# Attention into a mixture of experts on one core: gating of a batch cut into blocks and spread over later pairs' steps

## The chip, the cores and the metric

The kernel runs on one NeuronCore of a Trainium2 chip. The metric is the device time in microseconds (us); lower is better. The kernel before was run 14 times: median 584.34 us, from 579.7 to 599.25. One more execution was recorded by the hardware profiler: 582.62 us, of which 580.8 us lie between its first and its last instruction (the span).

## The reference

```python
q_d, k_d, v_d = (x.reshape(B, H, Sd, 4, D).mean(axis=3) for x in (q, k, v))
out_up = np.repeat(softmax_attn(q_d, k_d, v_d), 4, axis=2)
mask = np.abs(pos[:, None] - pos[None, :]) < 4
out_local = softmax_attn(q, k, v, mask)
x = (out_up + out_local)          # as 4608 rows (batch, position) of 512 (head, dim)
logits = x @ w_gate
e_idx = np.argmax(logits, axis=1)
gate_w = softmax(logits)[e_idx]
eom = sigmoid(x @ w_output_gate)
out[row] = gate_w * eom[row, e_idx] * (relu(x[row] @ w1[e_idx]) @ w2[e_idx])
```

There are 8 batches, 8 heads, 576 positions and 64 dims; 8 experts, with w1 512x1024 and w2 1024x512. Two attentions are added for each head: one over means of four positions, repeated four times, and one over a band of seven positions. The sum, all heads of a position side by side, is a row of 512; each row goes to the one expert that its logits choose.

## The kernel before, in words

Values go through TensorE as float16, the sensitive ones as a high half and a low half (the rest of the value after the high half), so that products come out nearly exact.

**Pairs.** The unit of attention is a pair of heads, u = 0 to 31; four pairs make a batch. For a pair, `load` (L178) issues six DMAs on SP's queue (q, k and v of two heads) and has POOL cast q and k to float16 (L187). `prep` (L195) makes v's halves `vh` on ACT (L201) and `vl` on DVE (L202), turns q and k on TensorE into the PSUM tiles `t1` and `t2f` (L214, L218), copies them out (L220, L221 on DVE, L223 on ACT), and forms v's means of four in `pd` (L229 to L232), with halves by ACT (L234) and DVE (L235). `scores_a` and `scores_b` (L248, L262) write a pair's masked scores to PSUM; `soft` (L241) makes the exponential's high half `eh` and the exponential itself on ACT (L244, L245), and the low half `el` on DVE (L246). `values` (L277) multiplies one head's exponentials with v in 27 matmuls into `po` (L298), and DVE divides by the row sums into the batch's tile `xo` (L301, L302).

**Gating.** When a batch's four pairs are through, its 576 rows lie in `xo` as five blocks of 120 rows (neighbours overlap). `gate1` (L304) repeats the coarse result four times by SBUF to SBUF DMAs on SP's queue (`up`, L313 to L316), adds it on POOL (L319), rounds to float16 on ACT (`xh`, L320) and takes the low half on POOL (`xl`, L321), each in one instruction of 120x2560 for all five blocks (for the last batch, one per block). `gate2` (L324) turns each block on TensorE into a PSUM tile `tp` (L331, L333), copies it out (L336 on ACT or L338 on DVE) and multiplies with the gate weights into a PSUM tile `lg` (L340, L343). `gate3` (L345) finds each row's expert and its rank there in some twenty small instructions, mostly on DVE, and POOL scatters the rows to DRAM, one indirect DMA for each block (L402). L392, in `gate3`, writes row numbers beside the rows.

**Experts.** From L509, one expert after another: its rows are read back, turned, and sent through two matmuls; POOL scatters the results to the output. Weights come on POOL's queue (`load_weights`, L158) into three sets of buffers; those of the first three experts are requested during attention, at u = 10, 16 and 22, each behind a one-element copy (L162, L163) that reads `vh` of that pair.

**PSUM.** [...] `T` has two slots shared by `t1`, `t2f`, `pd`, `lg`, `tp` and `gate3`'s rank tile; `SA` and `SB` (scores) take two banks each; `O` has two slots of one bank, one head's `po` each. `lg` keeps a slot of `T` from the first block of `gate2` until L350 has read it.

**Order.** [...] The compiler's scheduler sets that order: of the instructions that it takes to be ready, by its own model of time, the one written first. It also brings forward what is written much later, when that is ready. The loop at L423 writes, for each u: loads of u+3, `scores_a(u+1)`, head 0 of `values(u)`, `scores_b(u+1)`, `prep(u+2)`, head 1 of `values(u)`, and in the four steps after a batch `gate1`, `gate2` and `gate3` of that batch in the first, second and third.

Of the kernel before, what the change touches and what calls it, by code (L numbers as in the profile page):

```python
# [34 lines left out]
def kernel(  # L35
# [83 lines left out]
    for i in range(3):  # L119
        t_vh = cst.tile([128, 2, NB, 66], F16, tag=f"vh{i}")  # L120
        nc.vector.memset(t_vh[:, :, :, 64:66], 0.25)
        vh_s.append(t_vh)
        t_vd = cst.tile([128, 2, 2, 66], F16, tag=f"vd{i}")
        nc.vector.memset(t_vd[:, :, :, 64:66], 0.25)
        vdh_s.append(t_vd)
# [32 lines left out]
    def load_weights(e, after=None):  # L158
        w1sb = wpool.tile([128, 4, F], F16, tag="w1")
        w2sb = wpool.tile([128, NG, Dm], F16, tag="w2")  # L160
        if after is not None:
            nc.gpsimd.tensor_copy(w1sb[0:1, 0, 0:1], after)  # L162
            nc.gpsimd.tensor_copy(w2sb[0:1, 0, 0:1], after)  # L163
        nc.gpsimd.dma_start(w1sb, moe_w1[e].rearrange("(c p) f -> p c f", p=128))
        nc.gpsimd.dma_start(w2sb, moe_w2[e].rearrange("(g p) j -> p g j", p=128))
        wts[e] = (w1sb, w2sb)
# [9 lines left out]
    st = {}  # L176

    def load(u):  # L178

        b, hp = u // NP, u % NP  # L180
        s16 = []
        for i, src in enumerate((q, k)):
# [3 lines left out]
            t16 = sbA.tile([96, 6, 2 * D], F16, tag=f"qk16{i}")  # L186
            nc.gpsimd.tensor_copy(t16, f.rearrange("p m h d -> p m (h d)"))  # L187
            s16.append(t16)
# [4 lines left out]
        st[u] = {"s16": s16, "vf": vf}  # L193

    def prep(u):  # L195

        d = st[u]
        s16, vf = d.pop("s16"), d.pop("vf")
        vh = vh_s[u % 3]
        vl = sbA.tile([128, 2, NB, D], F16, tag="vl", bufs=3)  # L200
        nc.scalar.activation(vh[:, :, :, 0:D], vf, AF.Copy, scale=VS)  # L201
        nc.vector.scalar_tensor_tensor(vl, in0=vf, scalar=VS, in1=vh[:, :, :, 0:D],  # L202
                                       op0=ALU.mult, op1=ALU.subtract)
# [11 lines left out]
        for i in range(2):  # L215
            for m in range(6):
                c = 96 + SD * i + 24 * m
                nc.tensor.matmul(t2f[:, c:c + 24], lhsT=s16[i][:, m, :], rhs=pb[0:96, 0:24],  # L218
                                 start=True, stop=True)
        nc.vector.tensor_copy(qkT[:, 0:n1], t1[:, 0:n1])  # L220
        nc.vector.tensor_copy(qkT[:, n1:2 * S], t2[:, 0:2 * S - n1])  # L221
        qkd = sbA.tile([128, 2 * SD], F16, tag="qkd", bufs=3)
        nc.scalar.copy(qkd, t2f[:, 96:96 + 2 * SD])  # L223
        vdh = vdh_s[u % 3]
        vdl = sbA.tile([128, 2, 2, D], F16, tag="vdl", bufs=3)
        pd = psA.tile([128, 2, 2, D], F32, tag="T", bufs=2)
# [4 lines left out]
        for i, m in enumerate((vh, vl)):  # L231
            nc.tensor.matmul(pd[:, 1], lhsT=pv[:, NB - 1, 128:256], rhs=m[:, :, NB - 1, 0:D],  # L232
                             start=(i == 0), stop=(i == 1), skip_group_check=True)
        nc.scalar.copy(vdh[:, :, :, 0:D], pd)  # L234
        nc.vector.tensor_tensor(vdl, pd, vdh[:, :, :, 0:D], op=ALU.subtract)  # L235
        d.update(qT=qkT[:, 0:S], kT=qkT[:, S:2 * S], qd=qkd[:, 0:SD], kd=qkd[:, SD:2 * SD],
                 vh=vh, vl=vl, vdh=vdh, vdl=vdl)
        d["eh"] = sbA.tile([128, 2, ND], F16, tag="eh", name="eh", bufs=2)
        d["el"] = sbA.tile([128, 2, ND], F16, tag="el", name="el", bufs=2)

    def soft(d, ps, c0, c1):  # L241
# [4 lines left out]
        nc.vector.tensor_tensor(d["el"][:, :, c0:c1], ps[:, :, 0:n], d["eh"][:, :, c0:c1], op=ALU.subtract)  # L246

    def scores_a(u):  # L248
        d = st[u]
        ps = psA.tile([128, 2, 512], F32, tag="SA")  # L250
# [9 lines left out]
        soft(d, ps, 0, NA)  # L260

    def scores_b(u):  # L262
        d = st[u]
        ps = psA.tile([128, 2, 512], F32, tag="SB")
# [10 lines left out]
        soft(d, ps, NA, ND)  # L275

    def values(u, h, xo):  # L277

        d = st[u]
        eh, el = d["eh"][:, h], d["el"][:, h]  # L280
        hh = 2 * (u % NP) + h
        po = psA.tile([128, NB + 2, 65], F32, tag="O", bufs=2)
        mms = []
        for e_, hi in ((eh, True), (el, False)):
            for t in range(NB):
                c = slice(Q0[t], Q0[t] + 128)
                mms.append((po[:, t, 0:65], e_[:, c], d["vh"][:, h, t, 0:65]))
                if hi:
                    mms.append((po[:, t, 0:D], e_[:, c], d["vl"][:, h, t, :]))
            for g, q0 in ((NB, 0), (NB + 1, 16)):  # L290
                for kc, kn in ((0, 128), (1, 16)):
                    c = slice(S + SD * kc + q0, S + SD * kc + q0 + 128)
                    mms.append((po[:, g, 0:65], e_[0:kn, c], d["vdh"][0:kn, kc, h, 0:65]))
                    if hi:
                        mms.append((po[:, g, 0:D], e_[0:kn, c], d["vdl"][0:kn, kc, h, :]))

        for i, (o, a, m) in enumerate(mms):
            nc.tensor.matmul(o, lhsT=a, rhs=m, start=(i == 0), stop=(i == len(mms) - 1),  # L298
                             skip_group_check=True)
        rs = sbA.tile([128, NB + 2], F32, tag="rs", bufs=3)  # L300
        nc.vector.reciprocal(rs, po[:, :, 64])  # L301
        nc.vector.tensor_tensor(xo[:, :, D * hh:D * hh + D], po[:, :, 0:D], _bc(rs, D), op=ALU.mult)  # L302

    def gate1(b, parts):  # L304

        xo = xo_s[b]
        xh, xl = xh_s[b % 2], t_xl
        up = sbA.tile([BR, NB, Dm], F32, tag="up", bufs=1)
        for t in range(NB):
# [3 lines left out]
            nc.sync.dma_start(up[0:4 * n, t, :], _ap(src, [src.ap[0], [0, 4], [1, Dm]]))  # L313
            if n < 30:
                src = xo[112:128, NB + 1, :]
                nc.sync.dma_start(up[4 * n:BR, t, :], _ap(src, [src.ap[0], [0, 4], [1, Dm]]))  # L316
        for t0, t1 in parts:
            x = xo[0:BR, t0:t1, :]
            nc.gpsimd.tensor_tensor(x, x, up[:, t0:t1], op=ALU.add)  # L319
            nc.scalar.copy(xh[0:BR, t0:t1, 0:Dm], x)  # L320
            nc.gpsimd.tensor_tensor(xl[0:BR, t0:t1], x, xh[0:BR, t0:t1, 0:Dm], op=ALU.subtract)  # L321

    def gate2(b, ts):
        xh, xl = xh_s[b % 2], t_xl  # L324
        if ts[0] == 0:
            lg_s[b] = psA.tile([128, NB, 4 * E], F32, tag="T", name="lg", bufs=2)
        lg = lg_s[b]
        for t in ts:
            tp = psA.tile([128, 8, 128], F16, tag="T", bufs=2)
            for c in range(4):  # L330
                nc.tensor.transpose(tp[:, c, :], xh[:, t, 128 * c:128 * c + 128], id16)  # L331
            for c in range(4):
                nc.tensor.transpose(tp[:, 4 + c, :], xl[:, t, 128 * c:128 * c + 128], id16)  # L333
            xT = sbA.tile([128, 8, 128], F16, tag="xT")
            if t % 2:
                nc.scalar.copy(xT, tp)  # L336
            else:
                nc.vector.tensor_copy(xT, tp)  # L338
            for c in range(4):
                nc.tensor.matmul(lg[:, t, :], lhsT=xT[:, c, :], rhs=wg[:, c, :],  # L340
                                 start=(c == 0), stop=False, skip_group_check=True)
            for c in range(4):
                nc.tensor.matmul(lg[:, t, 0:2 * E], lhsT=xT[:, 4 + c, :], rhs=wg[:, c, 0:2 * E],  # L343
                                 start=False, stop=(c == 3), skip_group_check=True)

    def gate3(b):
        xh, w9, lg = xh_s[b % 2], w9_s[b % 2], lg_s.pop(b)
        P = BR
        lg2 = sbA.tile([P, NB, 4 * E], F32, tag="lg2")
        nc.scalar.copy(lg2, lg[0:P])  # L350
# [50 lines left out]
        for t in range(NB):  # L401
            ins = nc.gpsimd.indirect_dma_start(  # L402
                out=xs_dram.ap(), out_offset=bass.IndirectOffsetOnAxis(ap=pos[:, t:t + 1], axis=0),
                in_=xh[0:P, t, :].bitcast(I32), in_offset=None, bounds_check=E * REG - 1, oob_is_err=False)
# [3 lines left out]
    xo_s, lg_s = {}, {}  # L408
    NU = B * NP
    late = {10: 0, 16: 1, 22: 2}  # L410

    def late_weights(u):

        if u in late:
            load_weights(late[u], st[u]["vh"][0:1, 0, 0, 0:1])

    for u in range(3):
        load(u)
    for u in range(2):
        prep(u)  # L420
    scores_a(0)
    scores_b(0)
    for u in range(NU + 5):  # L423
        b, hp = u // NP, u % NP
        if u == 1:
            prefill()
        if u + 3 < NU:
            load(u + 3)
        if u + 1 < NU:
            scores_a(u + 1)  # L430
        if u < NU:
            if hp == 0:
                xo_s[b] = sbA.tile([128, NB + 2, Dm], F32, tag="xo", name="xo")
            values(u, 0, xo_s[b])
        if u + 1 < NU:
            scores_b(u + 1)
        if u + 2 < NU:
            prep(u + 2)
        if u < NU:
            values(u, 1, xo_s[b])  # L440
            late_weights(u)
        gb = b - 1
        last = gb == B - 1
        if gb >= 0:
            if hp == 0:
                gate1(gb, [(t, t + 1) for t in range(NB)] if last else [(0, NB)])
            if (hp == 1 and not last) or (hp == 0 and last):
                gate2(gb, [0, 1, 2, 3, 4])
            if (hp == 2 and not last) or (hp == 0 and last):
# [121 lines left out]
```

The softmax here doesn't subtract the row's maximum and nothing guards it: scores larger than these inputs give would overflow.

## Time and profile before

| | |
|---|---|
| median of 14 runs | 584.34 us |
| profiled execution | 582.62 us |
| its span | 580.8 us |
| setup until the first exponential (u = 0) | 0 to 14.75 us |
| the first exponential of u = 31 | 351.40 us |
| last scatter to the experts (L402) starts | 396.9 us |
| first result of the experts' first transposes copied (L481) | 406.5 us |
| busy: TensorE (PE) / DVE / ACT / POOL | 80% / 52% / 42% / 42% of the span |
| granted TensorE clock | 0.784 of full, mean |
| DMA moved | 81.68 MB, mean 141 GB/s |

How to read it: a window or timeline is in us from the span's start. In a line of windows an engine's entry is its busy time in that stretch with the number of its instructions, PEld is TensorE's weight loads, PEclk the granted clock as a share of full speed, DMA share the mean busy share of 16 DMA engines (several queues' packets overlap, so it can exceed 1). In a line of waits the engine and line ahead of the arrow waited for those behind it: us in total, times, longest. A bracket at a timeline's line is the idle time ahead of it and what ended that.

### The profile page before, as it was taken

The page shows a single profiled execution, that of the slowest core. Times are in us where ns is not written, and L with a number is a line of the kernel's source. Part 1 is how long each engine was busy: PE and PEld are TensorE (multiplying, and loading weights), DVE is VectorE, ACT ScalarE, POOL GpSimd, SP SyncE. Part 2 cuts the span into 40 slices and gives each one's busy share as a digit, 9 for nine tenths or more (in the row PEclk, how much of TensorE's full clock was granted, in tenths as well). Part 3 has the DMA queues.
Part 4 walks back from the last instruction along what each step waited for, and adds up shares of the span by engine and source line. Part 5 has one row for each costly group of instructions (what it writes and reads, how often), then busy time and mean ns, then how long its engine had stood idle before and what let it go on. Part 6 is the DMA issues. An engine that isn't in the chain of part 4 may idle for free.

```text
span 580.8 us, 12472 instructions
## 1 busy us (share of the span) xinstructions
PE 464.0 (80%) x5137; PEld 320.8 (55%) x5137; DVE 299.9 (52%) x604; ACT 244.6 (42%) x381; POOL 244.4 (42%) x227
## 2 busy tenths in 40 slices
PE   3988767786988987978888888240999969999992
PEld 2656546555766755755665666230655545665560
DVE  5665846864784774884684784530322222332230
ACT  1746535542652662644554554220233313333331
POOL 7203552942672662565365263743044223223212
PEclk9987955955775785777597597555899979999997
DMA  9999979886838963994951410314098987894201
GB/s 170 258 251 197 194 145 196 152 162 144 160 78 139 244 127 78 220 179 95 208 131 44 97 34 1 86 42 132 4 204 206 159 192 159 181 212 143 98 33 72
DMA packets 152563, 81.68 MB, mean 141 GB/s; under 512 B 121709, under 2 KB 140141, under 8 KB 152496
## 3 DMA queue, kind: packets, MB, share of 16 engines
q1 hardware_dynamic: 134832, 49.81, 41.6%
q0 software_dynamic: 17664, 30.98, 25.6%
q8 instruction: 42, 0.69, 0.5%
q14 instruction: 25, 0.20, 0.1%
HBM read 68.23 MB, written 20.72 MB: 153 GB/s over the span
## 4 chain that ended last, share of the span: by engine, by line
issue 30%; PE 25%; POOL 23%; SPq 6%; DVE 6%; DMA 5%; ACT 2%; POOLq 1%; ACTq 0%
PE po L298 7%; POOL out_dram L502 6%; POOL t_xl L321 6%; POOL xo L319 5%; POOL hx_xs L402 3%; PE pd L229 3%; POOL t L187 3%; SPq L149 2%; SPq L185 2%; PE tp L333 2%; PE pu L489 2%; PE t L214 2%; DMA vf<-in_v_dram 1%; DMA f<-in_k_dram 1%; PE tp L331 1%
## 5 line engine op out<-in xcount | busy, mean ns | idle before, releaser
L187 POOL CAST t<-f 96x768 f16<-96x768 f32 x64 | 56.0, 896 | 102.0 <-issue 54.8
L298 PEld LDWEIGHTS <-eh 128*128 128x128 f16 (+1 forms) x1152 | 59.5, 105 | 40.2 <-issue 19.1
L489 PE MATMUL pu<-xgT,w1sb 128*128 128x320 f16 x512 | 74.0, 307 | 1.8 <-DVE xgT L481 1.6
L499 PE MATMUL py<-w2sb,hs 128*128 128x512 f16 x320 | 70.4, 379 | 0.0
L246 DVE TENSOR_TENSOR el<-ps,eh 128x912 f16<-128x912 f32 x64 | 66.5, 1047 | 6.1 <-ACT ps L245 5.7
L502 POOL DMA_INDIRECT out_dram<-y,xg x40 | 39.4, 985 | 63.4 <-ACT y L501 61.5
L489 PEld LDWEIGHTS <-w1sb 128*128 128x128 f16 x512 | 51.3, 100 | 23.7 <-issue 2.8
L244 ACT ACTIVATE eh<-ps 128x912 f16<-128x912 f32 x64 | 57.1, 892 | 16.5 <-PE ps L257 13.6
L202 DVE SCALAR_TENSOR_TENSOR vl<-vf,t_vh 128x640 f16<-128x640 f32 x32 | 55.5, 1734 | 13.9 <-ACT t_vh L201 13.5
L492 ACT ACTIVATE hs<-pu 128x320 f16<-128x320 f32 x64 | 28.0, 437 | 76.2 <-PE pu L489 76.2
L402 POOL DMA_INDIRECT hx_xs<-t_xh,pos x40 | 41.4, 1035 | 39.9 <-DVE t_xh L390 23.1
L245 ACT ACTIVATE ps<-ps 128x912 f32<-128x912 f32 x64 | 57.0, 891 | 0.0
L321 POOL TENSOR_TENSOR t_xl<-xo,t_xh 120x2560 f16<-120x2560 f32 (+1 forms) x12 | 41.0, 3420 | 37.5 <-ACT t_xh L320 37.5
L481 DVE COPY xgT<-tp 128x1024 f16<-128x1024 f16 (+1 forms) x24 | 13.2, 597 | 80.8 <-PE tp L480 65.9
L494 DVE TENSOR_SCALAR hs<-pu 128x320 f16<-128x320 f32 x64 | 31.5, 492 | 44.5 <-PE pu L489 37.1
L298 PEld LDWEIGHTS <-el 128*128 128x128 f16 (+1 forms) x576 | 41.1, 104 | 21.4 <-issue 3.7
L319 POOL TENSOR_TENSOR xo<-xo,up 120x2560 f32<-120x2560 f32 (+1 forms) x12 | 45.5, 3793 | 16.8 <-DMA up<-xo 16.8
L298 PE MATMUL po<-t_vh,eh 128*128 128x65 f16 x320 | 37.0, 211 | 19.1 <-DVE xo L302 16.8
L499 PEld LDWEIGHTS <-hs 128*128 128x128 f16 x320 | 31.3, 98 | 36.5
L298 PE MATMUL po<-vdl,eh 128*128 128x64 f16 (+1 forms) x256 | 47.9, 206 | 0.0
L298 PE MATMUL po<-t_vd,eh 128*128 128x65 f16 (+1 forms) x256 | 47.9, 209 | 0.0
L501 ACT ACTIVATE y<-py,xg 128x512 f32<-128x512 f32 x40 | 27.5, 688 | 47.9 <-PE py L499 47.9
(118 smaller groups left out, 848.0 us busy)
## 6 DMA issues: line engine op xcount, KB each, us to landing
vf<-in_v_dram SPq DMA_DIRECT2D x64, 160.0 KB, 4.8
f<-in_q_dram SPq DMA_DIRECT2D x64, 144.0 KB, 4.3
f<-in_k_dram SPq DMA_DIRECT2D x64, 144.0 KB, 4.4
w1sb<-in_moe_w_dram POOLq DMA_DIRECT2D x8, 1024.0 KB, 9.7
w2sb<-in_moe_w_dram POOLq DMA_DIRECT2D x8, 1024.0 KB, 12.6
up<-xo SPq DMA_DIRECT2D x32, 240.0 KB, 4.2
hx_xs<-zt SPq DMA_DIRECT2D x8, 645.0 KB, 12.8
xg<-hx_xs SPq DMA_DIRECT2D x8, 645.0 KB, 5.0
```

Source lines behind the costliest of these rows:

```text
L187: nc.gpsimd.tensor_copy(t16, f.rearrange("p m h d -> p m (h d)"))
L202: nc.vector.scalar_tensor_tensor(vl, in0=vf, scalar=VS, in1=vh[:, :, :, 0:D], op0=ALU.mult, op1=ALU.subtract)
L244: nc.scalar.activation(d["eh"][:, :, c0:c1], ps[:, :, 0:n], AF.Exp, scale=scale)
L245: nc.scalar.activation(ps[:, :, 0:n], ps[:, :, 0:n], AF.Exp, scale=scale)
L246: nc.vector.tensor_tensor(d["el"][:, :, c0:c1], ps[:, :, 0:n], d["eh"][:, :, c0:c1], op=ALU.subtract)
L298: nc.tensor.matmul(o, lhsT=a, rhs=m, start=(i == 0), stop=(i == len(mms) - 1), skip_group_check=True)
L319: nc.gpsimd.tensor_tensor(x, x, up[:, t0:t1], op=ALU.add)
L321: nc.gpsimd.tensor_tensor(xl[0:BR, t0:t1], x, xh[0:BR, t0:t1, 0:Dm], op=ALU.subtract)
L402: ins = nc.gpsimd.indirect_dma_start(out=xs_dram.ap(), out_offset=bass.IndirectOffsetOnAxis(ap=pos[:, t:t + 1], axis=0), in_=xh[0:P, t, :] ...
L489: nc.tensor.matmul(pu[:, 0:c1 - c0], lhsT=w1sb[:, c, 128 * f:128 * f + 128], rhs=xgT[:, c, c0:c1], start=(c == 0), stop=(c == 3))
L499: nc.tensor.matmul(py, lhsT=hs[:, f, 128 * j:128 * j + 128], rhs=w2sb[:, f, :], start=(f == 0), stop=(f == NG - 1))
L502: ins = nc.gpsimd.indirect_dma_start(out=out_rows, out_offset=bass.IndirectOffsetOnAxis(ap=xgi[:, j, Dm // 2 + 1:Dm // 2 + 2], axis=0), in ...
```

## The change

The gating of a batch is cut into its five blocks, and each block's parts are written at later pairs' steps: `x_halves` (add, round, low half; 120x512 each) in the first to third step after the step that issues `up`, `x_turn` (transposes and their copy) one step later, `logits` one step later still. `logits` no longer has a PSUM tile of its own: it writes into columns 480 to 511 of the banks of the current pair's `po`, which is now one tile of two banks for both heads with a single buffer (before: two tiles of one bank), and ACT copies each block's logits out at once. `gate3` is written six steps after `up`, the scatters of single blocks one and two steps after that. What the last steps can't hold comes after the loop: batch 6's last logits, its `gate3` and scatters, three scatters of batch 5, and all of batch 7.

`prep` is cut into `cast`, `v_high`, `v_low`, `turn`, `v_means`, `v_means_low`. Loads are written four pairs ahead, the casts and v's halves three pairs ahead, with four `vh` and `vl` instead of three. The reciprocal of both heads is one instruction. The low half of the exponentials (`e_low`) is written apart from the exponentials. The one-element copies ahead of the weights' DMAs go, and the requests are written at u = 8, 14 and 20.

```diff
-    for i in range(3):
+    for i in range(4):
         t_vh = cst.tile([128, 2, NB, 66], F16, tag=f"vh{i}")
...
-    def load_weights(e, after=None):
+    def load_weights(e):
...
-        if after is not None:
-            nc.gpsimd.tensor_copy(w1sb[0:1, 0, 0:1], after)
-            nc.gpsimd.tensor_copy(w2sb[0:1, 0, 0:1], after)
...
+    def values(u):
+        d = st[u]
+        d["po"] = po2 = psA.tile([128, 2, 512], F32, tag="O", name="po")
+        for h in range(2):
+            po = po2[:, h, 0:65 * (NB + 2)].rearrange("p (t c) -> p t c", c=65)
...
+    def norm(u):
...
+        rs = sbA.tile([128, 2, NB + 2], F32, tag="rs")
+        nc.vector.reciprocal(rs, po[:, :, :, 64])
+        for h in range(2):
+            c = D * (2 * hp + h)
+            nc.vector.tensor_tensor(xo_s[b][:, :, c:c + D], po[:, h, :, 0:D], _bc(rs[:, h], D), op=ALU.mult)
...
-        for t0, t1 in parts:
-            x = xo[0:BR, t0:t1, :]
-            nc.gpsimd.tensor_tensor(x, x, up[:, t0:t1], op=ALU.add)
-            nc.scalar.copy(xh[0:BR, t0:t1, 0:Dm], x)
-            nc.gpsimd.tensor_tensor(xl[0:BR, t0:t1], x, xh[0:BR, t0:t1, 0:Dm], op=ALU.subtract)
...
+    def x_halves(b, t):
+        xh = xh_s[b % 2]
+        x = xo_s[b][0:BR, t, :]
+        nc.gpsimd.tensor_tensor(x, x, up_s[b][:, t], op=ALU.add)
+        nc.scalar.copy(xh[0:BR, t, 0:Dm], x)
+        nc.gpsimd.tensor_tensor(t_xl[0:BR, t], x, xh[0:BR, t, 0:Dm], op=ALU.subtract)
...
-        if ts[0] == 0:
-            lg_s[b] = psA.tile([128, NB, 4 * E], F32, tag="T", name="lg", bufs=2)
...
+    def logits(b, t, lg, fresh):
+        xT = st.pop(("xT", b, t))
...
+        nc.scalar.copy(lg_s[b][:, t, :], lg[0:BR])
...
-    late = {10: 0, 16: 1, 22: 2}
...
+    late = {8: 0, 14: 1, 20: 2}
+    def step(u):
+        b, hp = u // NP, u % NP
+        def parts(offs):
+            return [(g, t) for g in (b - 1, b - 2, b - 3) if g >= 0 for t in range(NB)
+                    if 4 * (g + 1) + offs[t] == u]
+        ex, tu, lo, sc = (parts(o) for o in ([1, 1, 2, 2, 3], [2, 2, 3, 3, 4], [3, 3, 4, 4, 5], [7, 7, 8, 8, 8]))
+        if u + 4 < NU:
+            load(u + 4)
+        if hp == 0 and b > 0:
+            upsample(b - 1, range(NB))
+        if u + 3 < NU:
+            v_high(u + 3)
+            cast(u + 3)
+        if u + 2 < NU:
+            turn(u + 2)
+        if u + 1 < NU:
+            scores_a(u + 1)
+        if u + 3 < NU:
+            v_low(u + 3)
+        values(u)
+        for i, (g, t) in enumerate(lo):
+            logits(g, t, st[u]["po"][:, i, 512 - 4 * E:512], False)
+        norm(u)
+        if u + 2 < NU:
+            v_means(u + 2)
+            v_means_low(u + 2)
+        if u + 1 < NU:
+            e_low(u + 1, 0)
+            scores_b(u + 1)
+        for i, (g, t) in enumerate(tu):
+            x_turn(g, t, i)
+        for g, t in ex:
+            x_halves(g, t)
+        if u + 1 < NU:
+            e_low(u + 1, 1)
+        for g, t in sc:
+            scatter(g, [t])
+        for g in (b - 1, b - 2):
+            if g >= 0 and 4 * (g + 1) + 6 == u:
+                gate3(g)
         if u == 1:
             prefill()
...
+        if u in late:
+            load_weights(late[u])
+        for u in range(4):
+            load(u)
+        for u in range(3):
+            cast(u)
+            v_high(u)
+            v_low(u)
+            if u < 2:
+                turn(u)
+                v_means(u)
+                v_means_low(u)
...
+        upsample(g, range(NB))
+        scatter(g - 2, [2, 3, 4])
+        scatter(g - 1, [0, 1, 2])
+        x_halves(g, 0)
+        scatter(g - 1, [3, 4])
+        for t in range(1, NB):
+            x_halves(g, t)
+        for t in range(NB):
+            x_turn(g, t, t % 2)
+            logits(g, t, psA.tile([128, 4 * E], F32, tag=("SA", "SB", "O")[t % 3], name="lg"), True)
+        gate3(g)
+        scatter(g, range(NB))
```

## The prediction, on record before the result

> **What bounds the kernel now.** First the page's slices, for where the time lies; then windows of 4 us, for what a stage is like; then the timelines and waits inside one stretch.
>
> ```profile
> PEclk9987955955775785777597597555899979999997
> ```
>
> Slices are 14.5 us. Attention is slices 1 to 25 and runs mostly at 5 to 8 tenths of the clock; the experts (from slice 29) run near full. The change touches only the first part.
>
> ```profile
> start us, us, engine line op out<-in xcount [idle before <-releaser]
> ...
> 47.23 0.93 ACT L244 ACTIVATE eh<-ps 128x912 f16<-128x912 f32 x1
> 54.68 0.93 ACT L244 ACTIVATE eh<-ps 128x912 f16<-128x912 f32 x1 [0.41 <-PE ps L257]
> 61.87 0.93 ACT L244 ACTIVATE eh<-ps 128x912 f16<-128x912 f32 x1 [0.41 <-PE ps L257]
> ```
>
> The first exponential of each pair is the pulse. Those of u = 4, 5, 6 come 7.2 to 7.4 us apart: the pace without gating, at full clock. The one of u = 31 comes at 351.40, so the 25 pairs from u = 6 take 289.5 us, 11.58 each. Gating therefore costs 4 x (11.58 - 7.2) = 17.5 us a batch, far more than its work. The windows show how (PE busy, PEld, DVE, ACT, POOL, then clock):
>
> ```profile
> 56.00:60.00 4.00, 3.40 (x64) 2.58 (x62) 2.68 (x4) 2.95 (x5) 1.65 (x2) 1.00 1.02 187
> ...
> 168.00:172.00 4.00, 4.00 (x49) 3.10 (x47) 2.73 (x3) 2.13 (x3) 3.46 (x2) 0.50 0.03 6
> 172.00:176.00 4.00, 4.00 (x41) 2.77 (x41) 3.56 (x6) 2.24 (x3) 0.30 (x2) 0.50 0.34 78
> ...
> 216.00:220.00 4.00, 1.50 (x29) 1.22 (x28) 2.32 (x5) 2.33 (x4) 4.00 (x2) 1.00 0.00 0
> 220.00:224.00 4.00, 4.00 (x45) 2.89 (x44) 2.35 (x3) 1.01 (x1) 1.68 (x3) 0.57 0.42 94
> 224.00:228.00 4.00, 3.82 (x43) 2.68 (x43) 2.19 (x5) 0.00 (x0) 0.00 (x0) 0.50 0.29 66
> 228.00:232.00 4.00, 1.99 (x27) 1.46 (x26) 1.50 (x3) 1.65 (x2) 0.00 (x0) 0.50 0.51 110
> ```
>
> Without gating 64 matmuls start in 4 us; while gating 27 to 45, at half clock, with DVE and ACT mostly idle. Two causes, from the timelines:
>
> ```profile
> 202.07 5.59 POOL L319 TENSOR_TENSOR xo<-xo,up 120x2560 f32<-120x2560 f32 x1
> ...
> 214.33 5.04 POOL L321 TENSOR_TENSOR t_xl<-xo,t_xh 120x2560 f16<-120x2560 f32 x1 [5.25 <-ACT t_xh L320]
> ```
> ```profile
> 204.62 3.78 DVE L202 SCALAR_TENSOR_TENSOR vl<-vf,t_vh 128x640 f16<-128x640 f32 x1
> ```
> ```profile
> ACT xT L336 <- PE tp L333: 69.4, 16, 7.2
> ...
> DVE xT L338 <- PE tp L333: 34.4, 15, 4.2
> ...
> PEld L340 <- DVE xT L338: 18.9, 18, 3.7
> ```
>
> First, POOL's long instructions: L202, 0.83 us when POOL rests, lasts until POOL's add is over, and everything behind it on DVE with it (mean of L202 in the stretch: 1.83 us). Second, `gate2`: `lg` holds one of the two slots of `T`, so the five blocks go through the other, transposes, copy, logits in turn (216 to 232 us), and no `t1`, `t2f`, `pd` of the next pair gets in.
>
> **The change, part by part.**
>
> *What a pair costs each engine, at full clock.* TensorE, by distances of starts near 200 to 208 us: values 2 x 1.6, `scores_a` 0.80, `scores_b` 0.83, turning 0.83, means 0.77: 6.4. Gating adds 0.7 a block and 0.4 for ranks, 3.9 a batch: 7.4 a pair in all. DVE: 0.83 + 1.10 + 1.00 + 0.65 + 0.25 + 0.42 + 0.20 + 2 x 0.62 = 5.7, and a batch 3 x 0.69 (L338) and 4.0 for `gate3` (its rows from 232.60 on): 7.2. ACT: 0.74 + 2 x 0.93 + 2 x 0.85 + 0.41 + 0.37 = 5.1, and a batch 5 x 0.62, 2 x 1.01, the logits' copies, 0.44: 6.7. POOL: casts 1.64, and a batch 5 x (1.26 + 1.15) and 5 scatters each 1.30: 6.3. SP issues six loads at about 0.48 and, a batch, 5.4 of `up`: 4.2. The DMAs bring a pair's loads in 4.9 us (POOL's casts wait for them at 47.6, 52.5 and 57.4), and `up` and scatters, 1.9 MB a batch at some 200 GB/s, add 2.4. Nothing is over 7.4.
>
> *Splitting.* Five adds of 1.26 and five low halves of 1.15 (the last batch's rows) are 12.0 for 10.6 before: 1.4 us more POOL a batch, covered, as POOL has some 4 us idle a batch even at 7.4 a pair. `vl` can now wait for one piece, at most 1.26, instead of 5.59. Logits' copies: five of 120x32 for one of 120x160 at 0.29; none of that size is in the trace; between 0.20 (120x5, L385) and 0.29: I take 0.22, 0.8 us more ACT a batch, inside the 6.7. The joint reciprocal saves one of 0.20 a pair; its 128x14 lies between 0.20 and 0.25. These decide nothing.
>
> *`lg` out of `T`.* This takes the 16 us passage away: turning and means get both slots back between blocks. Late next: `po`, single now. Values of u+1 wait until both divisions and the logits' copies of u are done; behind that wait stand means, scores and transposes of the same queue, 0.77 + 0.83 + 0.8 + 0.83 = 3.2 us that the scheduler can place ahead, against 0.2 + 2 x 0.62 = 1.4 us of DVE. Between nothing and 1.4 us a pair; 0.4 taken.
>
> *v, casts and loads earlier.* L202 and the casts leave the path to the next turning. Loads must land a pair's step earlier, but three buffers are free a step earlier too. I take nothing.
>
> *The pace* is then the 7.2 without gating plus the gating work of the fullest in-order engines, (3.1 + 2.0 + 1.1 + 0.4) / 4 = 1.6 on ACT, 1.5 on DVE, in which the 0.4 above is hidden or not: 8.8. Ends: 7.4, TensorE without a gap, and 11.58, nothing gained. Gain over 25 pairs: 25 x (11.58 - 8.8) = **69.5**, in it full clock, since no single wait should reach the length at which the rows lose it (216 to 221 us).
>
> *Clock, weighed.* In the rows above, half clock stays for 20 us though PE is 4.00 of 4.00 busy (168 to 176); it goes up after some 59 starts in 4 us (192 to 196, then 0.92). [...]
>
> *The weights' requests.* The copies that held them go. The order brings forward what is ready: L392 of the second batch that gates runs at 9.0 us.
>
> ```profile
> 9.01 0.88 DVE L392 TENSOR_SCALAR t_xh<-tok_i 120x5 int32<-120x5 int32 x2
> ```
> ```profile
> 109.70 5.89 SPq L185 DMA_DIRECT2D f<-in_k_dram  x2
> 116.41 6.13 SPq L192 DMA_DIRECT2D vf<-in_v_dram  x2
> ```
>
> The buffers are free from the start, so I expect all six requests in POOL's first gaps, 9 to 25 us, not at pairs 8 to 20. One expert's weights, requested at 106.8 and 109.2, landed about 121.7; beside them a load's issue went from 1.0 to 6 us. Some 170 GB/s moved in those 15 us, 2.5 MB, of which 2.1 weights, so loads lost about 12 us of transfer an expert, 36 for three, just where the DMAs are full anyway (share 1.0 to 1.3 until 57 us, prefill of `hx_xs` included). Loads run ahead of use by 9 us there (casts of u = 6 at 53, scores at 61.9). Cost: 36 - 9 = **27**. Ends: 0, if requests stay late, and 45, all three in a row with no load between. What was lost at 106, 176 and 246 us is in the 11.58 already.
>
> [...]
>
> *The tail.* Before, 55 us from the last pair's exponential to the experts' first copy, POOL's chain from 366.4 on deciding. After, three scatters of batch 5 come in, 3 x 1.3 = 3.9, partly in the wait for `up`: 0 to 4, I take **2**. The experts are as before.
>
> Sum against the profiled 582.62: -69.5 + 27 + 2 = -40.5, so 542; the median of runs is 1.7 above that execution, so **544**.
>
> **Rivals.**
>
> *Weights come late or cost nothing* (for: they are written at u = 8, 14, 20; against: the row at 9.01): 517.
>
> *Waits hand on.* A block crosses POOL, ACT, POOL, TensorE, DVE or ACT, TensorE, ACT. The scheduler works by a model, not by this trace; where it puts an ACT rounding ahead of an exponential and POOL is late, ACT stands. At a pace of 10.2 the gain is 34.5: about 579. For: ACT's and DVE's 69 and 34 us of waits for `tp` are of this kind. Against: the steps between parts.
>
> *Slower.* The same mechanism carried to the end: pieces are brought forward as L392 was, TensorE meets transposes whose low half isn't there, falls to half clock, and the pace stays 11.58; then weights and tail are all that is left: 582.6 + 27 + 2 + 1.7 = 613. It decides from a pace of 11.58 - 29 / 25 = 10.4 on.
>
> *The change doesn't do what it says:* the order is the scheduler's, so pieces may cluster though they are written spread; that is the case above.
>
> **How the numbers follow.** Forecast (525 to 562) 0.50; weights for nothing or a pace near 8 (500 to 525) 0.18; below 500 0.02; waits handed on (562 to 581) 0.13; within 0.5%, about what a measurement of this kernel can tell from no change, (581.4 to 587.3) 0.04; slower 0.13. Range 500 to 581 leaves out 0.19. Faster 0.83, same 0.04, slower 0.13.
>
> **What would show it.** L202 near 0.9 us mean; distance of L244's first exponentials 8 to 9.5 us; PEclk at 9 in most slices after the sixth; L164 and L165 starting before 30 us, and a gap in the exponentials before 80 us; `po` waits on L302's successor under 1 us a pair. Wrong would be: half clock through the middle, a pace over 10, or weights' requests after 60 us.

## The result and the profile after

The changed kernel takes 637.33 us, median of 10 runs (626.47 to 646.52), against 587.19 of the kernel before in 47 runs (577.09 to 602.4): a ratio of 1.087, 95% interval 1.081 to 1.093. It was forecast to be faster, at 544, and it is 8.7% slower.

The profiled execution of the changed kernel took 624.44 us, span 622.7. That is 41.8 above the profiled one of before and 12.9 below its own median; the account below is of these 41.8. Four of the runs below (e8, e10, e11, e15) were profiled in executions 1.5 to 2.4% above the fastest of the same kernel, so their paces and spans are upper ends.

The pulse is now at L258:

| | before | after | |
|---|---|---|---|
| first exponential, u = 0 | 14.75 | 14.77 | 0.0 |
| u = 6 | 61.87 | 89.14 | +27.3 |
| u = 6 to u = 31 | 289.5, 11.58 a pair | 298.9, 11.96 a pair | +9.4 |
| u = 31 to the experts' first copy | 55.1 | 59.1 | +4.0 |
| from there to the end | 174.3 | 175.5 | +1.2 |

The slices of the page after, the counterpart of those before (15.6 us each now):

```profile
PEclk9998659665588589575579675755599899899998
```

The clock falls from the fifth slice on (before from the sixth), and but for single slices it stays low through the middle, as it did before. Where the first 27 us went, in the timelines of POOL and of SP's queue, and ACT's pulse:

```profile
10.94 0.95 POOL L161 DMA_DIRECT2D w1sb<-in_moe_w_dram  x1
...
42.76 0.75 POOL L161 DMA_DIRECT2D w1sb<-in_moe_w_dram  x1
```
```profile
16.20 9.29 SPq L183 DMA_DIRECT2D f<-in_q_dram  x2
25.60 9.16 SPq L183 DMA_DIRECT2D f<-in_k_dram  x2
```
```profile
70.49 0.92 ACT L258 ACTIVATE eh<-psa 128x912 f16<-128x912 f32 x1
89.14 0.93 ACT L258 ACTIVATE eh<-psa 128x912 f16<-128x912 f32 x1
```

The six requests for weights go out between 10.94 and 43.51 us, between casts, and beside them two loads take 9 us to issue, which took 1.40 and 1.24 before. So the casts come late, and pair 6 with them.

The pace is another matter. VectorE's low half of v is cured (mean 0.97 us a piece for 1.73), yet the pace stayed. In the waits of the changed kernel (us in total, times, longest):

```profile
POOL t_xl L356 <- ACT t_xh L355: 113.7, 8, 20.6
...
PEld L224 <- POOL t L196: 34.7, 15, 5.8
...
PE t L224 <- POOL t L196: 29.8, 14, 4.9
```

One batch shows how the two belong together. First ACT, then POOL, then TensorE, each from its timeline:

```profile
232.39 0.85 ACT L258 ACTIVATE eh<-psb 128x816 f16<-128x816 f32 x1 [0.56 <-PE psb L295]
...
239.84 0.85 ACT L258 ACTIVATE eh<-psb 128x816 f16<-128x816 f32 x1 [1.87 <-PE psb L295]
...
242.28 1.13 ACT L355 CAST t_xh<-xo 120x512 f16<-120x512 f32 x2
```
```profile
224.66 2.49 POOL L354 TENSOR_TENSOR xo<-xo,up 120x512 f32<-120x512 f32 x2
242.97 1.29 POOL L356 TENSOR_TENSOR t_xl<-xo,t_xh 120x512 f16<-120x512 f32 x1 [15.82 <-ACT t_xh L355]
...
258.46 1.16 POOL L356 TENSOR_TENSOR t_xl<-xo,t_xh 120x512 f16<-120x512 f32 x1
259.56 3.89 POOL L196 CAST t<-f 96x768 f16<-96x768 f32 x5
```
```profile
257.30 0.66 PE L224 MATMUL t<-id,t 96*128 96x96 f16 x6 [4.94 <-POOL t L196]
```

POOL has two blocks added at 227.15. ACT's rounding of them stands, in ACT's order, behind two pairs' exponentials and runs at 242.28. POOL stands at the low half for 15.82 us. Behind it in POOL's order come the rest of the low halves, the adds, five scatters, and of the next pairs' casts one at 256.39 and then five from 259.56 on. The load that the first of these casts reads was issued by 226.90 us, and of the loads of q and k issued from 215 to 250 us none took longer than 5.2 us to land; so that cast stood behind the low half with its load there from some 232 us on. All gating is thus done in one lump while the casts wait, and TensorE stands for want of the cast q and k. The windows of that stretch (PE busy and starts, PEld, DVE, ACT, POOL, clock, DMA share, GB/s):

```profile
244.00:248.00 4.00, 3.88 (x64) 2.97 (x61) 3.50 (x10) 2.04 (x5) 4.00 (x5) 1.00 0.36 82
...
252.00:256.00 4.00, 0.36 (x1) 0.00 (x0) 1.62 (x3) 0.42 (x1) 3.09 (x4) 0.50 0.30 77
...
264.00:268.00 4.00, 4.00 (x44) 3.63 (x44) 2.07 (x3) 2.07 (x3) 0.00 (x0) 0.50 0.55 132
```

TensorE starts one matmul in 252 to 256 and has half clock until some 268.4 us. The step from u = 20 to u = 21 is 17.7 us; there is one such step a batch (17.5 to 20.2 us for u = 13, 17, 21, 25 and 29), and the others from u = 7 on are 6 to 15, where before one of 21 to 28 stood beside three of 5 to 13. The changed kernel still has one long stop a batch, with another cause.

### The profile page after: what moved, and what is told of

It reads as the page before. It is cut to its first block, busy times and chain, and to the rows that moved or that the text cites. A ratio compares the mean times of both kernels' runs of the same rounds, so it can differ in the third digit from the quotient of the medians.

```text
span 622.7 us, 12559 instructions
## 1 busy us (share of the span) xinstructions
PE 483.0 (78%) x5137; PEld 329.3 (53%) x5137; DVE 282.7 (45%) x574; ACT 251.3 (40%) x441; POOL 250.0 (40%) x277
## 5 line engine op out<-in xcount | busy, mean ns | idle before, releaser
L356 POOL TENSOR_TENSOR t_xl<-xo,t_xh 120x512 f16<-120x512 f32 x40 | 46.5, 1171 | 113.9 <-ACT t_xh L355 113.7
L196 POOL CAST t<-f 96x768 f16<-96x768 f32 x64 | 52.6, 845 | 98.1 <-DMA f<-in_q_dram 54.1
L321 PEld LDWEIGHTS <-eh 128*128 128x128 f16 (+1 forms) x1152 | 65.5, 112 | 30.4 <-issue 5.5
L224 PE MATMUL t<-id,t 96*128 96x96 f16 x320 | 31.6, 246 | 33.1 <-POOL t L196 29.8
L321 PE MATMUL po<-vdl,eh 128*128 128x64 f16 (+1 forms) x256 | 53.1, 222 | 0.0
L354 POOL TENSOR_TENSOR xo<-xo,up 120x512 f32<-120x512 f32 x40 | 51.8, 1307 | 2.9 <-DMA up<-xo 2.9
L321 PE MATMUL po<-t_vd,eh 128*128 128x65 f16 (+1 forms) x256 | 52.7, 220 | 0.0
L321 PEld LDWEIGHTS <-el 128*128 128x128 f16 (+1 forms) x576 | 40.2, 109 | 18.7 <-DVE el L265 1.5
L224 PEld LDWEIGHTS <-t 96*128 96x128 f16 x384 | 26.9, 119 | 43.5 <-POOL t L196 34.7
L242 PE MATMUL pd<-t_vh,pv 128*128 128x128 f16 x160 | 34.8, 280 | 14.0 <-DVE qkT L231 7.6
L321 PE MATMUL po<-t_vh,eh 128*128 128x65 f16 x320 | 40.1, 224 | 6.9 <-DVE xo L334 5.6
L321 PE MATMUL po<-t_vd,el 128*128 128x65 f16 (+1 forms) x256 | 43.7, 220 | 0.0
## 6 DMA issues: line engine op xcount, KB each, us to landing
w2sb<-in_moe_w_dram POOLq DMA_DIRECT2D x8, 1024.0 KB, 10.8
```

The lines of the kernel that those rows point to most:

```text
L224: nc.tensor.transpose(o, s16[i][:, m, :], id16[0:96, 0:96])
L242: nc.tensor.matmul(pd[:, 0], lhsT=pv[:, t, 0:128], rhs=m[:, :, t, 0:D], start=(i == 0), stop=(i == len(mms) - 1), skip_group_check=True)
L354: nc.gpsimd.tensor_tensor(x, x, up_s[b][:, t], op=ALU.add)
L356: nc.gpsimd.tensor_tensor(t_xl[0:BR, t], x, xh[0:BR, t, 0:Dm], op=ALU.subtract)
```

## The experiments

**Theory.** Two losses, both of order. (1) The weights' requests are early: 27 us. (2) POOL's queue stands at gating pieces that wait for another engine, and the next pairs' casts stand behind them. **Rivals.** The early weights disturb the loop too; the pieces' own work, the half clock or the single `po` sets the pace. The last is weak from the start: TensorE waited for `po` (L321 for L334) 5.6 us in all, in 8 waits, and 7.1 us in 4 for ACT's copies of the logits in it (L377 for L382).

All times are profiled ones, except the ratios, which are of repeated runs against the kernel before on the same chip, and where executions are named. The rows come from several chips; on those of e1 to e15 the kernel before had medians of 589.60 to 598.11 us, so rows whose spans lie a few us apart can't be ranked. "Clock" is TensorE's mean granted clock between the first exponentials of u = 6 and u = 31.

| run | u = 6 | pace | clock | span |
|---|---|---|---|---|
| before | 61.87 | 11.58 | 0.71 | 580.8 |
| after | 89.14 | 11.96 | 0.69 | 622.7 |
| e1 guard copies back | 68.19 | 12.15 | 0.65 | 603.3 |
| e2 rounding on POOL | 87.13 | 10.58 | 0.77 | 589.6 |
| e3 both | 65.51 | 11.41 | 0.69 | 594.1 |
| e4 before, requests early | 93.00 | 11.73 | 0.71 | 618.8 |
| e5 casts on DVE | 101.98 | 10.45 | 0.78 | 601.5 |
| e6 e2, guard on a cast | 65.47 | 10.98 | 0.74 | 580.7 |
| e7 e5, e2 and a guard | 74.12 | 11.92 | 0.65 | 614.7 |
| e8 before, add to low half in pieces | 74.40 | 12.02 | 0.62 | 605.2 |
| e9 ACT in program order | 103.55 | 10.14 | 0.79 | 591.4 |
| e10 all five in program order | 71.07 | 12.06 | 0.74 | 611.9 |
| e11 requests held by order | 77.44 | 12.10 | 0.66 | 617.9 |
| e12 e9 and e11 | 73.44 | 10.12 | 0.78 | 560.6 |
| e13 ACT and POOL in order | 71.12 | 10.55 | 0.76 | 575.6 |
| e14 e12 and rounding on POOL | 72.40 | 9.06 | 0.88 | 532.5 |
| e15 e14 without ACT's order | 71.62 | 11.32 | 0.68 | 594.0 |

**The weights: e1 and e4.** The one-element copies are put back, or taken out of the kernel before.

```diff
 # e1, on after (u = 8, 14, 20)
+        if after is not None:
+            nc.gpsimd.tensor_copy(w1sb[0:1, 0, 0:1], after)
+            nc.gpsimd.tensor_copy(w2sb[0:1, 0, 0:1], after)
-            load_weights(late[u])
+            load_weights(late[u], st[u + 2]["vh"][0:1, 0, 0, 0:1])
 # e4, on before
-    late = {10: 0, 16: 1, 22: 2}
+    late = {8: 0, 14: 1, 20: 2}
-            load_weights(late[u], st[u]["vh"][0:1, 0, 0, 0:1])
+            load_weights(late[u])
```

> The changed kernel with the one-element copies put back ahead of the weights' requests (they read the high half of v of pair u+2). Theory: the requests at 11 to 44 us cost the 27.3 us by which the first exponential of pair 6 came later (89.1 for 61.9), so this kernel is 22 to 28 us faster than the changed one, and pair 6 comes at 60 to 66 us; POOL's wait for ACT's rounding (113.7 us in all) stays near 110. Rival: the transfers are only displaced and cost the same in the middle; then pair 6 comes early, but the time falls by under 10 us.

> The kernel before with one part of the change alone: the one-element copies gone, the requests written at pairs 8, 14 and 20. Theory: the requests move to the first 50 us here too and delay the first pairs by some 27 us, of which the missing bursts in the middle give back little: 20 to 30 us slower than before, 605 to 615. Rival: 0 to 10 us slower, since before has stalls in the middle that the displaced transfers would leave shorter.

Measured: pair 6 starts 21.0 us earlier in e1 and 31.1 later in e4, the spans move by -19.4 and +38.0, and the pace hardly. By the profiled executions e1 gains 19.3 us, less than the 22 to 28 expected, and e4's 620.55 to 626.62 us lie above its 605 to 615. So the early requests do cost about what was forecast, somewhat less by e1 and more by e4, and most of it falls before pair 6. A guard has a price of its own, though: it makes POOL wait for ACT's `vh`, 34.1 us in three waits, the longest 16.1.

**The rounding: e2 and e3.** POOL makes the rounding itself and waits for nobody.

```diff
-        nc.scalar.copy(xh[0:BR, t, 0:Dm], x)
+        nc.gpsimd.tensor_copy(xh[0:BR, t, 0:Dm], x)
```

> The changed kernel with the rounding to the high half done by POOL instead of ACT, so that POOL works add, rounding and low half of a block without waiting for another engine. Theory: POOL stands up to 20 us a batch at the low half, with the casts of the next pairs behind it, and that holds the pace; then the wait goes, the pace from pair 6 to pair 31 falls from 11.96 to 10.3 us or less, and the time by 40 us or more. Rival: the single buffer of the pair's output with the logits in it, or the half clock, holds the pace; then the wait goes and the pace stays above 11.5, the time within 12 us of the changed kernel.

> Both edits together. Theory: the two costs lie in different places and add up: 65 us or more under the changed kernel, below 575, so faster than before. Rival on the weights: under 10 us better than the rounding on POOL alone. Rival on the pace: about the time of the first edit alone, 600 to 615.

Measured: e2 takes 33 us off the span and the pace falls to 10.58, though POOL got 40 instructions more (expected: 40 us and 10.3). But a step of 16 to 18 us a batch stays, now behind the first scatter. POOL's timeline of e2:

```profile
241.31 1.03 POOL L442 DMA_INDIRECT hx_xs<-t_xh,pos  x1 [8.48 <-DVE pos L436]
...
250.14 3.79 POOL L196 CAST t<-f 96x768 f16<-96x768 f32 x4
```

Four casts stand behind five scatters, and these behind VectorE's positions. e3 missed its expectation by 20 us: with both repairs the copies were the next thing to stand at (43.4 us in three waits, the longest 19.1), and one step took 32.6 us. With one wait taken away, the next one in the same queue showed.

**Out of the queue: e5, e6, e7.** The casts go to VectorE (e5); POOL rounds and the guard reads a tile that POOL itself has cast (e6); casts on VectorE, rounding on POOL and a guard (e7).

```diff
 # e5 and e7
-            nc.gpsimd.tensor_copy(t16, f.rearrange("p m h d -> p m (h d)"))
+            nc.vector.tensor_copy(t16, f.rearrange("p m h d -> p m (h d)"))
 # e6's guard, which is POOL's own product; e7's is vh_s[(u + 1) % 4]
+            load_weights(late[u], st[u + 3]["s16"][1][0:1, 0, 0:1])
```

> The changed kernel with the casts of q and k on DVE instead of POOL; the rounding stays on ACT and the requests early. Theory: POOL's standing costs only because the casts are queued behind it. So POOL may go on waiting 60 us and more for ACT's rounding and for the scatters' positions, and still the long step of each batch (17 to 20 us between two first exponentials) goes: pace from pair 6 to 31 at 10.3 us or less, the time 40 us or more under the changed kernel, though DVE gets some 1.2 us more a pair. Rival: the single output buffer with the logits holds the pace, DVE has more work: pace 11.5 or more, the time within 12 us of the changed kernel.

> The changed kernel with the rounding on POOL and the requests held back by one-element copies that read a cast tile of pair u+3, which POOL itself wrote, instead of v's high half, for which POOL stood 34 and 43 us in the two kernels before. Theory: the pace stays at the 10.6 of the rounding on POOL alone, pair 6 comes at 62 to 68 us instead of 87: 18 to 25 us under that kernel, a span of 565 to 572. Rival: the transfers cost in the middle what they spare at the start; then within 8 us of it.

> Casts on DVE, rounding on POOL, and the requests held back by copies that read the high half of v of pair u+1. Theory: with nothing of the next pairs left in POOL's queue, the pace goes to the 9 us that three of four steps have (7.6 to 8.8) plus DVE's casts, pair 6 comes at 62 to 68: 70 us or more under the changed kernel, below 560, faster than before. Rival: DVE becomes the bound with the casts on it: pace 10.5 or more, 575 and up.

e5 is the cleanest of these for the pace: POOL waits for the rounding even longer, but no cast stands behind, and the pace is 10.45. From its list of waits:

```profile
POOL t_xl L356 <- ACT t_xh L355: 125.2, 9, 19.7
```

A longer wait thus went with a shorter pace; what is queued behind it counted for more than its length. e5 still misses its expectation: 10.45 for 10.3, and 21 us off the span for 40, since pair 6 comes at 101.98 and two steps of 18 us remain. e6 is level with the kernel before (580.7 for 580.8), 9 over what was expected.

e7 missed by over 50, with no cast in POOL's queue either, so casts behind POOL's waits aren't the whole account. POOL waited at the guard again (42.4 us in two), and at scatters for the columns of `t_xh` that VectorE writes (40.6 in three). The casts, now VectorE's, came late as well; VectorE's timeline and TensorE's waits between 100 and 350 us in e7:

```profile
173.31 9.72 DVE L199 CAST t<-f 96x768 f16<-96x768 f32 x1
```
```profile
PE t L227 <- DVE t L199: 15.3, 9, 11.1
```

A cast of 0.55 us (median) lasted 9.72 while POOL, past its guard, worked gating instructions back to back from 169.78 to 182.61 us, and TensorE stood 11.1 us for it. The numbers of e7's rival (a pace of 10.5 or more, 575 and up) came true. But VectorE is busy for 69% of the time between pairs 6 and 31, so its work alone isn't the bound; single casts are held up (mean 0.84 us for 0.59 in e5). The rest of e7's 11.92 stays open.

**The splitting alone: e8.** The kernel before with add, rounding and low half in five pieces for every batch (`gate1(gb, [(t, t + 1) for t in range(NB)])`).

> The kernel before with one part of the change alone: its add, rounding and low half in five pieces for every batch, as it has them for the last. Theory: shorter POOL instructions shorten the low half of v on DVE (mean 1.83 us to 1.1 or less), but POOL now meets ACT's rounding five times with casts in between and behind, and the passage through the one free slot of the turning tiles stays: 570 to 590, pace 11 to 11.7. Rival: the long POOL instructions were the cause of the slow batches: pace under 10, 550 or less.

No gain: 593.66 at best, against 586.95 to 595.21 for the kernel before on the same chip. POOL's wait for the rounding rose from 37.5 us (longest 8.4) to 86.9 (longest 19.5). The low half of v did get shorter, 1.23 us in the mean for 1.73, so the long POOL instructions alone were not what made the batches slow. In pieces POOL stood there 14 times, where it had stood 7 times.

**The order alone: e9 and e10.** No work is changed; edges of issue order chain the loop's instructions of an engine in the order in which the program writes them. Without such edges the scheduler orders by its model of time.

```diff
         for u in range(NU):
+            n0 = len(traced)
             step(u)
+            pin(n0)   # each instruction of the chosen engines after the one traced before it
```

> The changed kernel; in the pairs' loop ScalarE's instructions are held to the order in which the program writes them (edges of issue order only, no work and no wait on another engine is added), so that a block's rounding stands ahead of the next pair's exponentials and no longer behind two pairs of them. Everything else is left to the scheduler, the early weights too. Theory (GpSimd's queue stands at a low half whose rounding is late in ScalarE's order): GpSimd's wait at L356 for L355 falls from 113.7 us to under 50, the pace from pair 6 to 31 from 11.96 us a pair to about 10.6, as when GpSimd did the rounding itself, pair 6 stays near 88 us, and the span is 585 to 600. Rival (the pace is set by the work of the pieces or by the one output tile po, and the wait is only where it shows): the wait moves, the pace stays between 11.5 and 12.2, the span between 610 and 630.

> The changed kernel; in the pairs' loop the instructions of all five engines' queues are held to the order in which the program writes them (issue order only), so that the weights' requests come where step 8, 14 and 20 write them, each block's rounding and low half stand in the step that writes them, and the scatters stand behind the casts of the steps before. No work is changed. Theory (both losses of the changed kernel are the order that the scheduler chose: weights early, and gating pieces bunched in GpSimd's queue ahead of casts): pair 6 begins at 62 to 66 us, the pace falls to 9.8 us a pair or less, the span is under 545. Rival (the spread pieces themselves, or the half clock, or the one po tile hold the pace, whatever the order): pair 6 at 62 to 66 us, since that part is the weights', but a pace of 11 to 12, and a span of 585 to 610.

e9 gives 10.14 us a pair, better than any change of work before it; as pair 6 came at 103.55 and not near 88, its ratio to before is still 1.004. The wait at L356 hardly fell (109.8 us), against the expectation, but it is now 20 waits for 8, and casts stand between them. e9, POOL's timeline:

```profile
230.95 2.27 POOL L356 TENSOR_TENSOR t_xl<-xo,t_xh 120x512 f16<-120x512 f32 x2 [3.83 <-ACT t_xh L355]
233.17 3.13 POOL L196 CAST t<-f 96x768 f16<-96x768 f32 x4
241.59 2.27 POOL L356 TENSOR_TENSOR t_xl<-xo,t_xh 120x512 f16<-120x512 f32 x2 [5.29 <-ACT t_xh L355]
```

TensorE's waits between 100 and 350 us in e9, where none for a cast is listed any more (in after 19.9 us, in nine):

```profile
PE tp L362 <- DVE qkT L233: 15.1, 6, 3.5
PE psa L274 <- DVE el L265: 14.2, 3, 7.0
```

e10 missed: program order everywhere is no better (12.06; 11.5 if all of the 14.3 us by which its profiled execution lies over the fastest fell into the loop). The casts come in time, but now TensorE's own queue stands. e10, TensorE's waits in the same stretch:

```profile
PE rk L401 <- DVE oh L399: 23.9, 5, 4.8
PE t2f L224 <- DVE rke L430: 19.1, 5, 4.6
```

Written in order, `gate3`'s rank matmuls stand ahead of the next pair's work until VectorE has the top choice, once a batch, and then the turning waits for the slot of `T` that the ranks hold. "The scheduler's order" as a whole is thus not what is bad, as I had put it for e10; the place of single pieces is.

**Which engine's order, and both repairs together: e11 to e15.** The requests are held in POOL's queue by an order edge behind the cast written ahead of them, so that nothing waits for another engine; ACT is held as in e9; in e13 POOL as well; in e14 and e15 POOL rounds.

```diff
+        prev = next(i for i in reversed(tc.nc.cur_bb.bb.instructions) if i.engine == mybir.EngineType.Pool)
         w1 = nc.gpsimd.dma_start(w1sb, ...)
         w2 = nc.gpsimd.dma_start(w2sb, ...)
+        # order edges, without a wait, from w1 and w2 to prev
```

> The changed kernel, with each of the three pairs of early weights' requests held in GpSimd's queue behind the cast that stands ahead of it in the program (issue order only, so no copy and no wait on another engine); all else is left to the scheduler. Theory (the early requests cost about 27 us ahead of pair 6 and no more): pair 6 begins at 61 to 66 us instead of 89.14, the pace from pair 6 to 31 stays between 11.4 and 12.0 us, the span is 593 to 603. Rival (the early weights also disturb the loop): the pace falls under 11, the span under 575.

> The same as the run with the weights' requests held in place, and ScalarE's instructions of the loop held to program order as well. Theory (two separate losses, both of order alone): pair 6 begins at 61 to 68 us, the pace is 10.0 to 10.5 us as with ScalarE's order alone (10.14), the span is 545 to 560, under the 580.8 of before. Rival (the pace of 10.14 was owed to the late start, with the loads well ahead): the pace returns to 11 or more and the span is over 575.

> The changed kernel with ScalarE's and GpSimd's instructions of the loop in program order, and TensorE's, VectorE's and SyncE's left to the scheduler. With all five in program order the pace was 12.06 us, and TensorE stood 24 us in five waits for VectorE's top choice ahead of the ranks' matmul and 19 us for its positions. Theory (it was TensorE's or VectorE's program order that made that pace, and GpSimd's does no harm): the pace is 10.0 to 10.6 us, pair 6 at 61 to 71, the span 545 to 570. Rival (GpSimd's program order, with a low half waiting right ahead of each pair's casts, is what made it): the pace is 11.5 or more and GpSimd waits 130 us or more at L356 for L355; span over 585.

> ScalarE's order and the weights' requests held as in the other run of this call, and the rounding of the blocks made by GpSimd itself in place of ScalarE, as in the second run. Theory (what is left of GpSimd's 110 us of waiting for the rounding still holds casts up): the pace falls under 9.8 us and the span under 545. Rival (with ScalarE in order that wait is already harmless, and GpSimd's added work of 40 roundings or its wait for the positions takes its place): the pace is 10.0 to 10.8 us, the span 550 to 575.

> As the best run so far (weights' requests held, rounding by GpSimd), but with ScalarE's order left to the scheduler again. In the recorded order of that program GpSimd's casts of the next pairs stand behind the first of a batch's scatters, which needs the positions; with ScalarE held, four casts stood ahead of it. Theory (what counts is which casts stand behind a waiting gating piece): TensorE waits for casts again, 10 us or more between 100 and 330 us, the pace is 10.3 to 10.8 as in the second run (10.58), the span 565 to 585. Rival (ScalarE's order no longer matters once it does no rounding, and what made 9.06 us was the rounding and the late weights together): the pace is 9.0 to 9.5, the span under 545.

e11: the requests go out from 110 us on; the pace stays (12.10), so the weights are not its cause. Pair 6 came at 77.44, though, 11 us later than expected: the scheduler moved other things as well, and only 11.7 of the 27.3 came back (the fill of `hx_xs`, for one, moved from 60.0 to 29.4 us, among the loads). e12: the two repairs add, span 560.6, ratio to before 0.965 (0.953 to 0.978); the pace of e9 was not owed to its late start. In e12 to e14 pair 6 stays some 10 us behind the kernel before. In e14 ACT's order puts the split of pair 6's v, which waits 8.87 us for its load, ahead of pair 4's exponentials; but e15, without ACT's order, has pair 6 at 71.62 as well, so the cause of these 10 us isn't shown. e13: POOL's program order does little harm (10.55; ratio 0.981), so e10's 12.06 came with the order of the other three, and the rows above name TensorE's. e14: 9.06 a pair, span 532.5, ratio 0.914 (0.906 to 0.922), the fastest of all; its median is 538.09. Its page and, from POOL's timeline, one batch:

```profile
PEclk9989689995987989968958855558999889999998
```
```profile
226.12 1.15 POOL L363 TENSOR_TENSOR t_xl<-xo,t_xh 120x512 f16<-120x512 f32 x1
227.67 0.82 POOL L203 CAST t<-f 96x768 f16<-96x768 f32 x1 [0.40 <-DMA f<-in_q_dram]
...
233.28 0.83 POOL L203 CAST t<-f 96x768 f16<-96x768 f32 x1 [0.15 <-DMA f<-in_k_dram]
239.60 1.34 POOL L449 DMA_INDIRECT hx_xs<-t_xh,pos  x1 [5.49 <-DVE t_xh L433]
```

The five blocks are added, rounded and lowered in a row, four casts follow as their loads land, and only then POOL stands at a scatter. e15 leaves ACT's order to the scheduler again, and then the first scatter stands ahead of casts, as POOL's timeline of e15 shows:

```profile
280.21 1.09 POOL L449 DMA_INDIRECT hx_xs<-t_xh,pos  x1 [7.70 <-DVE pos L443]
...
287.30 3.15 POOL L203 CAST t<-f 96x768 f16<-96x768 f32 x4
```

POOL waits 53.8 us for the positions (longest 17.1), the pace is 11.32, and the ratio 0.981 (0.974 to 0.989). If all that its profiled execution lies over the fastest, 12.4 us, fell into the loop, the pace would be 10.8, still some 1.8 above e14. TensorE's waits for casts were 5.9 us in it, fewer than the 10 expected, so that part of the chain isn't shown; ACT's order moves more than the casts.

## Why the prediction was wrong

- **The pace (8.8 us a pair, gain 69.5; measured 11.96, loss 9.4).** This is the step that failed, 79 of the 82 us by which the sum missed. "The 7.2 without gating plus the gating work of the fullest in-order engines" adds work and no waiting, on the ground that "no single wait should reach the length at which the rows lose" full clock. Waits of up to 20.6 us came, since I looked for what each piece costs and not for what stands behind it in its queue. The sum was not wrong about the work: with another order, and the rounding on POOL, e14 runs at 9.06 with the same pieces and the same single `po`. What the pace lost shows in the clock: pace times clock is 8.2 us a pair before, 8.3 after, 8.2 in e5, 8.0 in e9 and 8.0 in e14 (7.5 to 8.9 over all rows of the table), so the sum's 8.8 fits a loop at full clock, which these runs didn't get. TensorE's own waits for casts, 19.9 us between 100 and 350 us, are only a part of the 79; that the stops took the clock down is argued from their place in the windows, as no run sets the clock by itself.
- **The rival "slower" had the mechanism nearly right and its chance (0.13) too low.** Pieces did come out clustered and TensorE did starve; but not for the low halves (TensorE waited 9.2 us for them at L364) so much as for the casts behind them. Its 613 was 24 short of the median: 9 by the pace, 3 by the tail and the experts, and 11 by which the median lies further over the profiled execution than before.
- **The weights (27; measured 27.3).** Right in kind, and the reason with it: e4 alone brings +31.1. That it came out to 0.3 us is luck: putting the guard back gave 21.0 in e1, holding the requests by order 11.7 in e11, and the requests spread to 43.5 us, not 25.
- **Splitting, `po`, v.** L207 fell to 0.97 (forecast near 0.9), waits for `po` to 0.2 us a pair, 0.4 with those for the logits' copies (0.4 taken). Right, and worth little while another wait took the place of theirs.
- **The tail (+2; measured +4.0, and +1.2 in the experts).** Right in kind.

Left open: why the changed kernel's other runs take 12.9 us (median) longer than the profiled one; how much of a long stop is the stop and how much the half clock after it, which no run here separates; and what besides late casts slowed e7 and e15.

## What to carry to other kernels

When work moves in an engine's queue, list for each moved piece what it may wait for on another engine and what then stands behind it (in after, casts behind a wait of 15.82 us); the length of the wait matters less than whether the next stage's input is in that list (e5: a longer wait, and a pace 1.5 us shorter). A program's spread is no spread in the queues: look at the order that the scheduler recorded, and hold single engines by order edges where its model is wrong, not all of them. A one-element copy used as a guard was a wait of its own (e1: 34.1 us in three); an order edge held the requests back to 110 us in e11 without a copy.

## What the runs showed of the hardware

Half clock outlasted the stop in after. Behind it, TensorE is 4.00 of 4.00 us busy at clock 0.50 in the window 264 to 268 of after, shown above. The next four windows:

```profile
268.00:272.00 4.00, 3.43 (x58) 2.30 (x56) 1.41 (x4) 3.18 (x8) 0.60 (x1) 0.95 0.87 210
272.00:276.00 4.00, 3.28 (x52) 2.58 (x53) 4.00 (x7) 2.35 (x3) 4.00 (x5) 0.90 0.88 166
276.00:280.00 4.00, 4.00 (x48) 3.22 (x47) 0.97 (x2) 0.41 (x2) 1.26 (x2) 0.50 1.25 217
280.00:284.00 4.00, 4.00 (x45) 2.35 (x43) 3.04 (x7) 2.67 (x5) 0.00 (x0) 0.50 0.33 49
```

From 276 on the clock is at 0.50 again with 4.00 of 4.00 busy, though the two windows ahead had 0.95 and 0.90 and were only 0.57 and 0.72 us idle. The stretches differ in length: in after, the busy stretch began at 263.7 and the clock rose some 4.7 us later; in the rows 168 to 176 of before, in the prediction, 8 us of full busy time stayed at 0.50. The loss at 276 came with 1.3 us idle in the 8 us ahead of it. What sets these lengths is not shown.

In e7 an instruction lasted many times its usual length beside another engine: VectorE's cast of 96x768, 0.55 us in the median, took 9.72 us while GpSimd worked without a gap (169.78 to 182.61 us).

The same wait on POOL, 110 to 125 us in all, went with paces of 11.96 (after), 10.45 (e5) and 10.14 (e9). Its total didn't say what it cost.
